# An attention-plus-GLU kernel takes its instruction order and buffer places from a stored table, and most closing waits move ahead of the last four stores

## Chip, cores and metric

The kernel runs on one core of one Trainium2 chip. A core has five engines that each take their instructions in the order of their own queue: TensorE (PE, matrix products), VectorE (DVE), ScalarE (ACT), GpSimd (POOL) and SyncE (SP, which here only starts transfers). They meet through semaphores. The metric is device time in microseconds (us) of one execution; less is better.

## What is computed

Sequence S = 2048, width D = 512, H = 32 heads of 16, feed-forward width F = 1792, all bfloat16.

```python
xn  = layernorm(x)                                   # no scale, no shift
qkv = xn @ wqkv                                      # 512 x 1536
p   = softmax(q @ k.T / 4)                           # per head, 2048 x 2048
a   = (p @ v) @ wo
h   = relu(xn @ W_gate) * (xn @ W_up)
out = x + a + h @ W_down
```

## The kernel before

**Tiles and units.** The 2048 queries are cut into four chunks of 512 (`c4`), the 32 heads into four groups of eight (`gg`), and each group into two blocks of four heads (`ee`). For each of the 32 blocks the kernel walks over 16 key tiles of 128 keys. A key tile of a block is 4 heads x 128 keys x 512 queries of scores. Most key tiles are two *units*: a unit is two heads, whose scores fill two PSUM banks, and one ScalarE instruction (`ACTIVATE ring<-ps`, line 1419) takes the exponential of both banks into a slot of `ring`. There are 720 units. The other 152 key tiles are *quads*: VectorE turns the four banks of scores into integers that are exponentials when they are read as bfloat16 (`qd<-ps`, line 1372), and VectorE or GpSimd makes two shifted copies (lines 1392 and 1388).

**Two halves of TensorE.** Nearly all products use tiles of 64 rows by 32 columns. A *group* is four such instructions side by side in columns, with 512 columns of data, on the upper or the lower 64 rows: half 0 or half 1. All of them are issued by the helper `matmul_loaded` (line 122). The weights of a group are loaded before it by four `LDWEIGHTS` instructions (lines 846, 1324 and 1352), except where the group before it on the same half used the same weights: then the four loads are left out (`wkey`, and `held` in `emit`). The scores of a unit are one group on each half. Behind them in the same queue stand the products with v (`ring,v_aug` and `qd,v_aug`), the projections of q, k and v, the gate, up and down products of the feed-forward part and the output projection.

**Order.** The program is first recorded as a graph of 8,000-odd operations (`Graph.op`). `Graph.run` is a list scheduler: it holds the candidates of each engine, gives each a start time from assumed durations and slacks, and always places the one that can start first, with rules for urgent scores and for weights that can stay. It also gives each tile its buffer (`slot_for`) and puts filler products into idle time at the start. `Graph.emit` then turns dependences into semaphore waits and writes out the five queues in that order.

**Scores and exponentials.** Unit u uses one of two pairs of PSUM banks (`ps`, four banks for units, four for everything else), so its scores have to wait until the exponential of unit u-2 has read them. TensorE can be ahead of ScalarE by one unit, no more.

**End.** SyncE starts all 459 transfers. Each kind of transfer has semaphores of its own, 102 in all. At the end of SyncE's queue `play` waits on every one of them, behind the last four stores (`out_dram<-xn_sb`, line 1221):

```python
            if e == "SP":
                for s, v in fin:
                    eng.wait_ge(s, v)
```

In the compiled program two of these waits share an instruction (line 550, 51 instructions). The output rows of those stores come from a chain behind the last exponential: the last block's sum is normalised on VectorE (lines 1192 to 1199), multiplied by the last part of `wo`, added to the residual (lines 1213 and 1216) and stored.

Of the kernel before, what the change touches and what calls it, by code (L numbers as in the profile page):

```python
# [1 line left out]

# [11 lines left out]
S = 2048  # L14
D = 512
H = 32
DH = 16
F = 1792
# [3 lines left out]
NB = 4  # L22
# [12 lines left out]
D_STEP = 3  # L35
W_LEAD = 34
# [53 lines left out]
NHS = 20  # L90

# [35 lines left out]
class Graph:  # L127
# [67 lines left out]
    def run(self):  # L195
        ops = self.ops
        for o in ops:
            o.users = []
        for o in ops:
            if o.after is not None and int(o.after) > 0:  # L200
                o.order.add(self.units[min(int(o.after), len(self.units)) - 1])
            pre = set(o.deps) | o.order
            o.left = len(pre)
            for d in pre:
                d.users.append(o)
        cand = {e: [] for e in self.ENGS}
        free = {e: 0.0 for e in self.ENGS}
        self.queue = {e: [] for e in self.ENGS}
        for o in ops:
            if o.left == 0:  # L210
                cand[o.eng].append(o)
        n = 0

        def slot_for(t):

            best, second = None, None
            for i in (t.allowed if t.allowed is not None else range(len(t.pool.cur))):
                c = t.pool.cur[i]
                if c is None:
                    at = 0.0  # L220
                else:
                    us = c.w + c.r
                    if not all(u.done for u in us):
                        continue
                    at = max(u.end for u in us)
                if best is None or at < best[0]:
                    best, second = (at, i), best
                elif second is None or at < second[0]:
                    second = (at, i)
            if t.pool.shared:  # L230
                held = any(c is not None and c.open > 0 for c in t.pool.cur)
                if t.extra:
                    if t.extra.slot is None:
                        return None
                elif t.open:
                    if held and not (self.EARLY and second is not None):
                        return None
                elif len(t.allowed) > 3 and (not held or any(b.slot is None and b.extra.slot is not None for b in self.twins)):
                    return second
            return best  # L240


        pe = {"mode": "full", "at": -1e9, "free": [0.0, 0.0]}
        last = {}

        def ready(o):
            at = 0.0
            for d in o.deps:
                at = max(at, d.end if d.eng == "PE" else d.end + ((0.0 if d.urgent else max(self.DMA_SLACK, o.slack)) if d.eng == "SP" else o.slack))
            for d in o.order:  # L250
                at = max(at, d.start if d.eng == o.eng else d.end)
            for t in o.acq:
                if t.slot is not None:
                    continue
                b = slot_for(t)
                if b is None:
                    return None
                at = max(at, b[0] + (o.slack if o.eng == "SP" else 0.0))
            return at

        def pe_start(o, at):

            if o.mode != "half" or pe["mode"] != "half":
                st = max(at, max(pe["free"]) + (self.SWITCH if o.mode != pe["mode"] else 0.0), pe["at"] + self.ISSUE)
            else:
                st = max(at, pe["free"][o.half], pe["at"] + self.ISSUE)
            was = last.get(o.bank) if o.mode == "half" else None
            if was is None or was.half == o.half:
                return st, None
            return max(st, was.end + 25.0), was  # L270

        held = [None, None]

        def pick_pe():
            found = []
            for o in cand["PE"]:
                at = ready(o)
                if at is not None:
                    found.append((pe_start(o, at)[0], o))
            if not found:  # L280
                return None
            urgent = [(st, max(st, free["ACT"] - self.FILL - 60.0) if o.urgent == 2 else ready(o) + 120.0 if o.urgent > 2 else st + 216.0, o) for st, o in found if o.urgent]
            first = min(st for st, o in found)

            def fits(st, o):
                if o.urgent:
                    return True
                for su, by, q in urgent:
                    if o.mode == q.mode and o.half != q.half:
                        if st > by:  # L290
                            return False
                    elif st + o.dur + (self.SWITCH if o.mode != q.mode else 0.0) > by:
                        return False
                return True
            best = None
            for st, o in found:
                if not fits(st, o):
                    continue
                key = (st > first + self.NEAR, st if st > first + self.NEAR else 0.0,
                       o.prio - (self.REUSE if o.half is not None and o.wkey == held[o.half] else 0.0), o.idx)  # L300
                if best is None or key < best[0]:
                    best = (key, st, o)
            return best[1:]


        port = {"DVE": (0.0, None), "POOL": (0.0, None)}

        def pick(e):
            if e == "PE":
                return pick_pe()  # L310
            got = None
            for o in cand[e]:
                at = ready(o)
                if at is None:
                    continue
                at = max(at, free[e])
                if o.port:
                    at = max(at, port["POOL" if e == "DVE" else "DVE"][0])
                late = at > free[e] + 1e-6
                key = (late, at if late else 0.0, o.prio, o.idx)  # L320
                if got is None or key < got[0]:
                    got = (key, at, o)
            return None if got is None else got[1:]

        wire = 0.0
        while n < len(ops):
            best = None
            got_pe = None
            for e in self.ENGS:
                got = pick(e)  # L330
                if e == "PE":
                    got_pe = got
                if got is not None and (best is None or got[0] < best[0]):
                    best = (got[0], e, got[1])
            if got_pe is not None and best[1] == "PE":
                at, o = got_pe
                kind = None
                for f in self.fillers:
                    t = f[0].cur[f[1]]
                    if t is not None and t.name == f[2] and any(u.done for u in t.w):  # L340
                        kind = f
                        break
                if kind is not None:
                    idle = max(pe["free"])
                    before = self.SWITCH if pe["mode"] != kind[4] else 0.0
                    room = at - idle - before - (self.SWITCH if o.mode != kind[4] else 0.0)
                    dur = 216.0 * (self.COLD if idle < self.WARM_AT else 1.0)
                    if room >= dur + 14.0:
                        f = Op()
                        f.eng, f.dur, f.fn, f.prio, f.name, f.mode, f.half, f.bank, f.urgent = "PE", dur, kind[3], 0.0, "fill", kind[4], None, None, 0  # L350
                        f.lat, f.stream, f.after, f.deps, f.order, f.acq, f.users = self.LAT["PE"], None, None, {}, set(), [], []
                        f.load, f.wsrc, f.wkey, f.wwaits, f.pair = None, (), None, (), None
                        f.idx = len(ops) + self.nfill
                        self.nfill += 1
                        f.start = idle + before
                        f.end = f.start + f.dur + f.lat
                        f.done = True
                        f.seq = len(self.queue["PE"])
                        self.queue["PE"].append(f)
                        pe["mode"], pe["at"], pe["free"] = kind[4], f.start, [f.start + f.dur] * 2  # L360
                        continue
# [61 lines left out]
    def emit(self, nc, es):  # L423
# [20 lines left out]
        for e in self.ENGS:  # L444
            n = {}
# [1026 lines left out]
```

## Time and profile before

| what | us |
|---|---|
| median of 3 runs (lowest, highest) | 695.87 (694.74, 700.77) |
| span of the profiled execution | 696.8 |
| first exponential of a unit starts | 11.4 |
| last exponential of a unit starts | 684.2 |
| ACT busy / PE busy / DVE busy / POOL busy | 671.8 / 678.8 / 603.4 / 504.2 |
| weight loads busy (beside PE) | 385.5 |

The profiled execution has no other time on record than its span, which is 0.9 us over the median of the runs and inside their range. In the rows of the profile, "busy" is the union of an engine's instructions; "PEld" is the weight load beside the products; a bracket behind a row gives the idle time ahead of it and what ended it, and "issue" there means that nothing which the profile shows was waited for. A matrix product lasts 375 ns in the rows, but the next group on the same half starts 216 ns after it, since they overlap in the pipeline. The granted TensorE clock is 1.00 in every stretch of the main part.

### The profile page before, as it was taken

To read this page: it belongs to the slowest core of one execution; us is meant where nothing else is said; L and a number is where in the kernel's file an instruction comes from. 1 tells how busy PE (TensorE), PEld (TensorE's weight loads), DVE (VectorE), ACT (ScalarE), POOL (GpSimd) and SP (SyncE) were. 2 spreads that over 40 slices of the span, in tenths; PEclk is the share of its full clock that TensorE was granted. 3 is DMA by queue.
4 is the path that set the end of the run, shared out by engine and by line. 5 is a ranking of instruction groups with operands and counts; after the bars stand their busy time and mean duration, and the time that the engine had idled before them with its cause. 6 is when DMAs were issued, how large, how long until landed. Compare 5 with 4: busy or idle time off the path is not lost.

```text
span 696.8 us, 46210 instructions
## 1 busy us (share of the span) xinstructions
PE 678.8 (97%) x22229; PEld 385.5 (55%) x20884; DVE 603.4 (87%) x1009; ACT 671.8 (96%) x733; POOL 504.2 (72%) x511
## 2 busy tenths in 40 slices
PE   8999999999999999999999999999999999999996
PEld 4556565555654656455655455654655575655663
DVE  9958899999899688888999887899999788899875
ACT  6999999999999999999999999999999999999994
POOL 3323759767689786868979787787778886786871
PEclk9999999999999999999999999999999999999999
DMA  7330312153201121211211121122210121221001
GB/s 212 71 65 6 92 46 63 46 140 96 63 27 40 41 80 55 52 47 56 68 35 33 41 78 49 49 62 58 58 54 25 48 72 50 62 58 40 27 17 48
DMA packets 65736, 40.65 MB, mean 58 GB/s; under 512 B 19912, under 2 KB 61576, under 8 KB 65544
## 3 DMA queue, kind: packets, MB, share of 16 engines
q1 hardware_dynamic: 65544, 37.69, 19.8%
q8 instruction: 169, 2.77, 1.7%
q14 instruction: 23, 0.19, 0.1%
HBM read 31.06 MB, written 2.35 MB: 48 GB/s over the span
## 4 chain that ended last, share of the span: by engine, by line
PE 62%; ACT 33%; DVE 2%; issue 1%; SPq 0%; DMA 0%; DVEq 0%
PE ps L122 61%; ACT ring L1419 32%; DVE qd L1372 1%; PE ps L950 1%; SPq L1288 0%; DVE xn_sb L775 0%; DVE v_aug L911 0%; DMA x_sb<-oT 0%; PE ps L800 0%; ACT qT L993 0%; PE ps L1434 0%; PE ps L968 0%; ACT xnT L808 0%; PE ps L1175 0%; DVEq L552 0%
## 5 line engine op out<-in xcount | busy, mean ns | idle before, releaser
L1419 ACT ACTIVATE ring<-ps 128x1024 bf16<-128x1024 f32 x720 | 665.5, 1102 | 8.5 <-PE ps L122 7.3
L1388 POOL TENSOR_TENSOR qd<-qd,ints 128x512 int32<-128x512 int32 x450 | 454.7, 1042 | 148.8 <-DVE qd L1392 58.7
L122 PE MATMUL ps<-qT,kT 64*32 64x512 bf16 x8192 | 463.5, 375 | 4.1 <-issue 0.9
L1372 DVE TENSOR_SCALAR qd<-ps 128x512 int16<-128x512 f32 x608 | 395.6, 684 | 56.5 <-PE ps L122 51.5
L122 PE MATMUL ps<-qd,v_aug 64*32 64x512 bf16 x3648 | 294.1, 375 | 1.3 <-issue 1.2
L122 PE MATMUL ps<-ring,v_aug 64*32 64x512 bf16 x2880 | 249.9, 375 | 0.5
L1352 PEld LDWEIGHTS <-kT 64*32 64x32 bf16 x7972 | 171.8, 92 | 123.8 <-issue 35.6
L1324 PEld LDWEIGHTS <-v_aug 64*32 64x32 bf16 x5400 | 131.8, 92 | 73.7 <-issue 18.6
L122 PE MATMUL ps<-xnT,wus 64*32 64x512 bf16 x1792 | 138.3, 375 | 1.1 <-issue 1.1
L122 PE MATMUL ps<-xnT,wgs 64*32 64x512 bf16 x1792 | 136.8, 375 | 0.6 <-issue 0.5
L1392 DVE TENSOR_SCALAR qd<-qd 128x2048 int16<-128x2048 int16 x79 | 62.8, 803 | 0.5
L846 PEld LDWEIGHTS <-wgs 64*32 64x32 bf16 x1792 | 44.1, 92 | 26.0 <-issue 5.8
L122 PE MATMUL ps<-Wd,hT 64*32 64x512 bf16 x768 | 56.8, 375 | 1.3 <-DVE qd L1372 0.5
L846 PEld LDWEIGHTS <-hT 64*32 64x32 bf16 x1792 | 44.2, 92 | 23.9 <-issue 4.9
L846 PEld LDWEIGHTS <-wus 64*32 64x32 bf16 x1792 | 44.1, 92 | 24.0 <-issue 5.5
L1057 DVE COPY up_sb<-ps 128x512 f32<-128x512 f32 x56 | 38.2, 683 | 4.6 <-PE ps L122 4.4
L122 PE MATMUL ps<-Wv,hT 64*32 64x512 bf16 x512 | 41.4, 375 | 0.8 <-issue 0.7
L1061 DVE SCALAR_TENSOR_TENSOR hT<-ps,up_sb 128x512 bf16<-128x512 f32 x56 | 38.2, 681 | 4.3 <-PE ps L122 4.0
L122 PE MATMUL ps<-Wk,hT 64*32 64x512 bf16 x512 | 40.5, 375 | 0.0
L122 PE MATMUL ps<-Wo_p,x_sb 64*32 64x512 bf16 x480 | 37.8, 375 | 0.0
L122 PE MATMUL ps<-xnT,Wq 64*32 64x512 bf16 x480 | 36.7, 375 | 0.2 <-issue 0.2
L122 PE MATMUL ps<-xnT,Wk 64*32 64x512 bf16 x480 | 34.2, 375 | 0.2 <-DVE xnT L816 0.2
(72 smaller groups left out, 267.4 us busy)
## 6 DMA issues: line engine op xcount, KB each, us to landing
rb<-rec_scr SPq DMA_DIRECT2D x31, 256.0 KB
wus<-in_B_W_up_dram SPq DMA_DIRECT2D x56, 128.0 KB, 3.1
wgs<-in_B_W_gate_dram SPq DMA_DIRECT2D x56, 128.0 KB, 2.8
xr_sb<-in_A_x_dram SPq DMA_DIRECT2D x16, 128.0 KB, 3.1
out_dram<-xn_sb SPq DMA_DIRECT2D x16, 128.0 KB, 1.8
qT<-qf SPq DMA_DIRECT2D x120, 16.0 KB, 2.8
x_sb<-in_A_x_dram SPq DMA_DIRECT2D x8, 128.0 KB, 2.6
x_sb<-oT SPq DMA_DIRECT2D x60, 16.0 KB, 2.6
```

The source lines that it names most:

```text
L122: return e.add_instruction(mybir.InstMatmult(name=e.bass.get_next_instruction_name(), engine=mybir.EngineType.PE, ins=[e.lower_ap(x), e.lo ...
L846: e.ldweights(w()[rows, 32 * j:32 * j + 32], tile_position=(rows.start, 32 * j))
L950: ins = e.matmul(ps[:, BANK[0], :], Wo_l[:, 0, 0:128], zeros, start=True, stop=True)
L1057: G.op("DVE", 603, lambda e: e.tensor_copy(up_sb[:, tup.slot, :], bank_of(tu)), reads=[tu], writes=[tup], prio=-590)
L1061: G.op("DVE", 603, lambda e: e.scalar_tensor_tensor(out=hT[:, th.slot, :], in0=bank_of(tg), scalar=0.0, in1=up_sb[:, tup.slot, :], op0=ALU ...
L1324: e.ldweights(vs(j), tile_position=(64 * half, 32 * j))
L1352: e.ldweights(ks(m), tile_position=(64 * half, 32 * m))
L1372: G.op("DVE", 601, lambda e, j=j, tx=tx: e.tensor_scalar(qd[:, tq.slot, 512 * j:512 * j + 512], ps[:, BANK[tx.slot], :], IBIAS[3], 0.0, op ...
L1388: G.op("POOL", POOL_NS / POOL_PIECES + 60, lambda e, x=x, n=n, c=slice(i * m, i * m + m): e.tensor_tensor(x().bitcast(I32)[:, c], raw().bi ...
L1392: G.op("DVE", 600, lambda e, n=n, x=x: e.tensor_scalar(x(), raw(), float(SHIFTS[n + 1]), None, op0=ALU.add), reads=[ti, tq], writes=[t], p ...
L1419: exp_ops[u] = G.op("ACT", 904, lambda e, tr=tr, k0=k0: e.activation(ring[:, tr.slot, :, :], ps[:, 4 * k0:4 * k0 + 2, :], ACTF.Exp, scale= ...
```

## The change

The list scheduler in `Graph.run` is taken out. A string of some 14 KB holds, packed, the operation that stands at each of 8,281 places of a common order and the buffer of each tile; `run` unpacks it and fills the five queues from it. No duration, slack or priority is read any more. Dependences that come from buffers being used again are worked out from the table as before; for transfers that share a semaphore, a wait for a user of the one before is added. In `emit`, the closing waits on the transfers that are not among the last four are put ahead of the first of these four.

The graph itself, the kernels' operations, the sizes, the split between engines and the buffers' number are the same. The two compiled programs have the same count of every instruction on ACT, DVE, POOL and SP, and the same matrix products; of weight loads there are 20,764 before and 19,660 after.

```diff
+LAST_STORES = 4
...
+PLAN_OPS = 8281
+PLAN = (
...
     def run(self):
-        ops = self.ops
...
-        def slot_for(t):
...
-        def pick_pe():
...
-        def pick(e):
...
+        ops, n = self.ops, len(self.ops)
+        plain = zlib.decompress(base64.b85decode(PLAN))
+        m = PLAN_OPS
+        self.queue = {e: [] for e in self.ENGS}
+        at, places = -1, iter(plain[2 * m:])
...
+        for i in range(m):
+            at += plain[i] * 256 + plain[m + i] - 65536 * (plain[i] > 127)
+            o = ops[at] if at < n else self.blank(at)
             for t in o.acq:
                 if t.slot is not None:
                     continue
+                t.slot = next(places)
+                c = t.pool.cur[t.slot]
                 if c is not None:
                     for u in c.w + c.r:
+                        assert u in placed
+                        if u.eng != o.eng or o.eng not in ("PE", "ACT"):
                             o.deps[u] = True
+                t.pool.cur[t.slot] = t
+            if o.eng == "SP":
+                for e in self.ENGS:
+                    us = [u for u in users.get(ahead.get(o.stream), ()) if u.eng == e and u is not o and o not in u.deps]
+                    if us:
+                        u = min((u for u in us if u in placed), key=lambda u: u.seq)
+                        if e != "SP":
+                            o.deps[u] = True
+                ahead[o.stream] = o
...
+            o.seq = len(self.queue[o.eng])
+            self.queue[o.eng].append(o)
+            placed.add(o)
         ops += [o for o in self.queue["PE"] if o.name == "fill"]
...
+                if e == "SP" and i == len(self.queue[e]) - LAST_STORES:
+                    late = {id(q.sem[0]) for q in self.queue[e][i:]}
+                    for s, v in fin:
+                        if id(s) not in late:
+                            eng.wait_ge(s, v)
                 wait(o.waits)
                 ins = o.fn(eng)
...
             if e == "SP":
                 for s, v in fin:
-                    eng.wait_ge(s, v)
+                    if id(s) in late:
+                        eng.wait_ge(s, v)
```

## The prediction

> **What bounds the kernel now.** First the page: busy times, instruction queues and the row of the exponentials.
>
> ```profile
> PE 678.8 (97%) x22229; PEld 385.5 (55%) x20884; DVE 603.4 (87%) x1009; ACT 671.8 (96%) x733; POOL 504.2 (72%) x511
> ...
> q8 instruction: 169, 2.77, 1.7%
> ...
> PE 62%; ACT 33%; DVE 2%; issue 1%; SPq 0%; DMA 0%; DVEq 0%
> ...
> L1419 ACT ACTIVATE ring<-ps 128x1024 bf16<-128x1024 f32 x720 | 665.5, 1102 | 8.5 <-PE ps L122 7.3
> ```
>
> ACT and PE both look full, and the chain of waits changes between them. Which of them limits is read from the starts of the 720 exponentials. The first starts at 11.4 us, the last at 684.2: 672.8 us for 719 steps. The commonest and shortest step is 0.904 us, and 719 x 0.904 = 650.0, so ACT is late by 22.8 us in all; 84 steps are over 0.95 us. An order can't shorten the 0.904. It can win back lateness, and something of the 11.4 us ahead or the 12.6 us behind.
>
> Next, where the lateness arises: the timeline around one of the longest pauses.
>
> ```profile
> 152.39 0.10 PEld L846 LDWEIGHTS <-wus 64*32 64x32 bf16 x3
> 152.56 0.38 PE L122 MATMUL ps<-ring,v_aug 64*32 64x512 bf16 x4
> 153.75 0.09 PEld L846 LDWEIGHTS <-wus 64*32 64x32 bf16 x1 [1.26 <-issue]
> 153.75 0.39 PE L122 MATMUL ps<-xnT,wus 64*32 64x512 bf16 x4 [0.81 <-issue]
> ...
> 154.64 1.02 ACT L1419 ACTIVATE ring<-ps 128x1024 bf16<-128x1024 f32 x1 [0.90 <-PE ps L122]
> ```
>
> A group of four weight loads is broken after the third, PE stands still for 1.18 us (152.56 to 153.75) with nothing to wait for, and the next exponential is 0.90 late. Counting PE's rows in the timeline, this pause stands at row 9,150, and every pause of this kind has the same remainder, 190, when its row is divided by 256. The page says why that is no accident: q8 moved 2.77 MB of instructions in 169 packets, PE ran 22,229 + 20,884 = 43,113, so 64 bytes each and one packet per 256. PE pauses where the next packet is not there. The packet ahead of this pause began at 150.89 and had landed at 152.31, and PE went on 1.4 us after that. Over the run PE loses 22.9 us at these borders, 15.05 of them in 25 pauses over 0.3 us. Of ACT's 22.8 us of lateness, 14.1 lie around the 36 pauses over 0.25 us, and 8.7 elsewhere.
>
> Last, the end of SP's queue: the closing waits, and the last four stores.
>
> ```profile
> L550 SPq EVENT_SEMAPHORE  x51: 17/28/28, 693.3 to 696.3; - x51
> ...
> L1221 SPq DMA_DIRECT2D out_dram<-xn_sb x4: 350/442/511, 691.1 to 692.8; - x4
> ...
> DMA to landing us min/median/max: 1.8/1.9/1.9
> ```
>
> 51 instructions from 693.29 to 696.39 are 61 ns each. The last store, issued at 692.77, has landed at about 692.77 + 1.9 = 694.7; the waits go on for 1.7 us after that.
>
> **The change, part by part.**
>
> *Closing waits.* 49 of the 51 instructions go ahead of the first of the last four stores. Queued behind them there are only these four. SP's issue before is at 679.78 (`rb`, line 1271); its landing is what GpSimd's last product (line 1279) waits for, until 684.79. If SP is held that long and then needs 49 x 61 ns = 3.0 us, it is free at 687.8, and the first store's data come at 691.15: 3.3 us of cover. Two instructions are left behind the last landing. Gain 1.7 - 0.1 = **1.6 us**; without the cover, up to 3.0 us would stand ahead of the stores, a loss of 1.4.
>
> *Fewer weight loads.* The change's order lets the same weights stand for two groups more often: 20,764 loads written out become 19,660, so 1,104 instructions or 4.3 packets of 256 less. The loads themselves lie beside products and cost nothing there; what counts is how long a packet lasts. I count matrix products per packet in both orders and set beside it what PE lost in the trace of before:
>
> | products in a packet | before: packets, us lost, pauses over 0.3 us | after: packets |
> |---|---|---|
> | 129 or less | 41, 4.2, 5 | 13 |
> | 130 to 135 | 100, 17.1, 19 | 62 |
> | 136 or more | 21, 1.3, 0 | 82 |
>
> With the same loss per packet in each row, after has 13 x 5/41 + 62 x 19/100 = 13.4 long pauses for 24, and 1.3 + 10.6 + 4.9 = 16.8 us lost for 22.5. Of ACT's 14.1 us near pauses this saves 44% by the number of long ones (6.2 us) or 25% by the sum (3.6 us). I take **6.2 us**, since the lateness was found at long pauses, and keep 0 and 14.1 as bounds.
>
> The page "Runtime: NRT & Kernel Launch" of the Trainium skill ("Instruction fetch mechanics") has blocks of 256 instructions too, but calls the crossing mostly hidden, because dispatch is slower than the fill. By that, this term would be 0 and the time that of the first rival below; the pauses above speak against it.
>
> *Where the groups stand.* Between the scores of one unit and the next, 0.904 us have room for 8.4 groups (216 ns each, two halves). Units with nine or more: 124 before, 200 after, which is worse. Four units in a row with 33 or more: 188 before, 148 after, which is better. Giving each window the mean lateness that such a window has in the trace, ACT's sum goes from 22.4 to 23.6 us by single units, to 22.3 by fours, to 20.7 by eights. I take **0**, and +1.2 and -1.7 as ends.
>
> *Neighbours on the same half.* In program order, 779 groups stand behind one of the same half before, 1,640 after. If the other half may run past a group that waits for its own half, this costs nothing. In the trace it may: of 5,528 groups, 136 begin more than 30 ns before the group that stands ahead of them in the program, 135 of these on the other half. Cost 0; the second rival is the case that it doesn't hold.
>
> *Other queues.* The orders of ACT, of DVE up to its 50th instruction and of PE up to its tenth exponential are the same, so the 11.4 us stay. Products on VectorE's and GpSimd's shifted copies: GpSimd's stand 6 units (before 7) ahead of their reader in the median, 3 (4) at least. Two pieces are 2 x 1.04 us, 2.3 units: still hidden, by less. SP's transfers are mixed anew: gate and up weights now stand at least 8 units, 7.2 us, ahead of their load (up: 10 before), with 3.1 us to landing. The extra waits on transfers with a shared semaphore hold SP only, and fewer of its instructions carry a wait (166, before 208). All of these **0**; if SP is held for the 7.5 to 12.8 us that its longest waits for DVE now take, the weights' cover is gone and a stall of some us follows once or twice. At the end three more groups on half 0 stand behind the last scores, beside 4.4 us in which PE waits for VectorE; bound 3 x 0.216 = 0.6 us.
>
> *Sum*, against the span: 696.8 - 1.6 - 6.2 = 689.0. The runs' median is 0.9 lower: **688.1 us**.
>
> **Rivals.**
>
> *Only the end is faster.* The pauses move to other places and stay as many, for a packet of 136 products lasts 136/8 x 0.216 = 3.7 us at full speed, and one of 132 no less than 3.6. For: four of the long pauses came behind packets that had lasted 3.9 us and more. Against: no long pause in 21 packets of 136 or more. Time 695.9 - 1.6 = 694.3.
>
> *The halves go in program order.* Then a group that waits for its half holds the other half too. Making pairs of neighbours on different halves, the order has 2,920 steps before and 3,052 after, 132 x 0.2155 = 28.4 us more of PE, for 651 us of exponentials a total of 658 us and 16.8 us of pauses. With PE on the chain for 62% of the span, 17.6 us of it reach the end: 695.9 + 17.6 - 1.6 - 6.2 = 705.7; all of it, with no gain at the packets, 722.7. It decides from 7.8 us, 27% of the 28.4. Against are the 136 early groups; for it is that only few places in the trace show it, since before has only half as many such neighbours, and hardly three in a row without a wait. The page "TensorE: Matmul & The Clock Gate" of the Trainium skill ("The mechanism" of tiling) states this rule outright: products start and end strictly in program order, only weight loads are pulled ahead. By it this rival is the forecast; the trace disagrees in the 136.
>
> *Most lateness goes.* Half of the 8.7 us elsewhere go as well, and nearly all of the 14.1: 695.9 - 1.6 - 14.1 - 4.4 = 675.8. For: the order is not bound to starting the earliest first, and no bound stands in the way above 672. Against: pauses can't all vanish with 62 packets in the middle row.
>
> *The waits at the end do harm*, as worked out: 697.3 if nothing else gains.
>
> **How the numbers follow.** Forecast (682 to 692 by its terms' ends around 688) 50%; only the end 18%; program order 16%; most lateness 14%; harm at the end 2%. The range leaves out half of the fourth case at the bottom and most of the second at the top: 676 to 704. One per cent is 7 us, about what a measurement of this kernel can tell from no change: faster means under 688.9, slower over 702.8. Faster: 36 of the forecast's 50 and the 14 of most lateness, 0.50; the same: 14 + 18, and 2 for harm at the end, with 2 of program order, 0.36; slower: 14 of program order, 0.14.
>
> **What will show it.** The waits: two semaphore instructions behind the last landing, the end about 2 us after the last store's issue. The packets: some 165 on q8, and 13 or so pauses over 0.3 us at equal remainders of 256. The halves: if program order rules, PE's rows show the second half starting with the second of two neighbours, and ACT's lateness grows evenly, far from packet borders. Wrong would be the forecast if the exponentials' steps near borders are as late as before, or if ACT waits for DVE or transfers in places where it now doesn't.

## The result and the profile after

The changed kernel is slower by about half a per cent: 699.32 us median of 20 runs (697.04 to 702.00) beside 696.50 of 20 of the kernel before (692.56 to 700.77), ratio 1.0045 with a 95% interval of 1.0029 to 1.0060. Two further measurements, on chips 2 and 14, gave 1.0054 and 1.0050. The forecast was 688.1, so about 11 us are missing; 699.32 lies inside its range, on the side of the second rival. The profiled execution took 700.15 us, with a span of 698.4.

| | before | after |
|---|---|---|
| start to first exponential, us | 11.4 | 11.7 |
| first to last exponential | 672.8 | 675.8 |
| last exponential to end | 12.6 | 10.8 |
| pauses at packet borders: us in all (of these over 0.3 us) | 22.9 (25) | 9.8 (9) |

The end is 1.8 us shorter and the pauses are less than half, and still the stretch of exponentials is 3.0 us longer. First the page of the changed kernel, with the lines that answer to those of before:

```profile
PE 685.9 (98%) x22232; PEld 359.8 (52%) x19780; DVE 598.3 (86%) x1009; ACT 674.8 (97%) x733; POOL 503.2 (72%) x511
...
q8 instruction: 164, 2.69, 1.6%
...
PE 80%; ACT 14%; SPq 2%; DVE 1%; DMA 1%; issue 1%; DVEq 0%
...
L1357 ACT ACTIVATE ring<-ps 128x1024 bf16<-128x1024 f32 x720 | 668.4, 1060 | 8.5 <-PE ps L227 6.7
```

The instruction queue has five packets fewer (169 before). The chain of waits lies on PE for 80% instead of 62%. The idle time ahead of the exponentials is 8.5 us as before, which misleads: the records of two exponentials that follow each other overlap, so an exponential that comes 0.1 us late leaves no idle time at all. Lateness has to be read from their ends (further down). The view of waits gives PE's time without a cause, `issue`: us in all, times, longest. Before and after:

```profile
PE ps L122 <- issue: 5.0, 12, 0.8
```

```profile
PE ps L227 <- issue: 1.0, 3, 0.4
```

That is the saving at the packet borders, as far as this view sees them. And the end of SP's queue, by line (durations in ns, then when the first and the last started):

```profile
L478 SPq EVENT_SEMAPHORE  x48: 28/28/28, 688.2 to 691.1; - x48
...
L1159 SPq DMA_DIRECT2D out_dram<-xn_sb x4: 350/388/437, 694.7 to 696.1; - x4
...
DMA to landing us min/median/max: 1.7/1.8/1.8
...
L488 SPq EVENT_SEMAPHORE  x2: 17/22/28, 697.4 to 697.9; - x2
```

The closing waits end at 691.1, 3.6 us before the first of the last stores; two of them stand behind the last landing. The compiled program packs them into 50 instructions, 51 before; PE, DVE, ACT and GpSimd carry some more semaphore instructions than before too (PE 135, before 116), which e5 below leaves as they are.

### The profile page after: what moved, and what is told of

It is laid out like the page before. It is cut to its first block, busy times and chain, and to the rows that moved or that the text cites. A ratio compares the mean times of both kernels' runs of the same rounds, so it can differ in the third digit from the quotient of the medians.

```text
span 698.4 us, 45138 instructions
## 1 busy us (share of the span) xinstructions
PE 685.9 (98%) x22232; PEld 359.8 (52%) x19780; DVE 598.3 (86%) x1009; ACT 674.8 (97%) x733; POOL 503.2 (72%) x511
## 4 chain that ended last, share of the span: by engine, by line
PE 80%; ACT 14%; SPq 2%; DVE 1%; DMA 1%; issue 1%; DVEq 0%
PE ps L227 79%; ACT ring L1357 14%; DVE qd L1310 1%; SPq L832 1%; DMA wus<-in_B_W_up_dram 1%; SPq L1226 1%; PE ps L888 1%; PE ps L1372 0%; DMA x_sb<-oT 0%; SPq L982 0%; PE ps L738 0%; PE ps L906 0%; ACT xnT L746 0%; DVEq L490 0%; PE ps L1113 0%
## 5 line engine op out<-in xcount | busy, mean ns | idle before, releaser
L227 PE MATMUL ps<-qT,kT 64*32 64x512 bf16 x8192 | 470.8, 374 | 2.0 <-issue 0.6
L227 PE MATMUL ps<-qd,v_aug 64*32 64x512 bf16 x3648 | 265.8, 375 | 0.1
L227 PE MATMUL ps<-ring,v_aug 64*32 64x512 bf16 x2880 | 242.2, 375 | 0.7 <-issue 0.4
L1290 PEld LDWEIGHTS <-kT 64*32 64x32 bf16 x7560 | 158.0, 92 | 123.0 <-issue 37.3
L1262 PEld LDWEIGHTS <-v_aug 64*32 64x32 bf16 x4708 | 113.4, 91 | 77.1 <-issue 25.1
L784 PEld LDWEIGHTS <-hT 64*32 64x32 bf16 x1792 | 41.3, 92 | 29.3 <-issue 6.5
L1330 DVE TENSOR_SCALAR qd<-qd 128x2048 int16<-128x2048 int16 x79 | 53.9, 690 | 0.5
L227 PE MATMUL ps<-Wv,hT 64*32 64x512 bf16 x512 | 46.2, 375 | 0.1
L227 PE MATMUL ps<-Wk,hT 64*32 64x512 bf16 x512 | 44.7, 375 | 0.0
```

The lines of the kernel that those rows point to most:

```text
L227: return e.add_instruction(mybir.InstMatmult(name=e.bass.get_next_instruction_name(), engine=mybir.EngineType.PE, ins=[e.lower_ap(x), e.lo ...
L784: e.ldweights(w()[rows, 32 * j:32 * j + 32], tile_position=(rows.start, 32 * j))
L1262: e.ldweights(vs(j), tile_position=(64 * half, 32 * j))
L1290: e.ldweights(ks(m), tile_position=(64 * half, 32 * m))
L1330: G.op("DVE", 600, lambda e, n=n, x=x: e.tensor_scalar(x(), raw(), float(SHIFTS[n + 1]), None, op0=ALU.add), reads=[ti, tq], writes=[t], p ...
```

## The experiments

Ratios are to the kernel before on the same chip; 1% is 7 us. "Late" is, of one profiled execution, the sum over the 719 steps from the end of one exponential to the end of the next, less 0.9165 us each (the last section says where that comes from), "near" what of it lies up to some 4 us behind pauses over 0.25 us at packet borders (with a stretch of 2 us, up to 2 us of it would count as "elsewhere" instead).

| kernel | chip | ratio to before (95%) | late, us: near + elsewhere | pauses, us (over 0.3) |
|---|---|---|---|---|
| before | | 1 | 11.2 + 2.8 | 22.9 (25) |
| after | | 1.0045 (1.0029 to 1.0060) | 4.1 + 12.8 | 9.8 (9) |
| e1_waits_alone | 2 | 0.9983 (0.9965 to 1.0001) | 10.3 + 2.1 | 20.8 (26) |
| e2_loads_back | 2 | 1.0108 (1.0077 to 1.0140) | 2.4 + 16.6 | 8.8 (8) |
| e3_cap9 | 2 | 1.0043 (1.0023 to 1.0062) | 3.8 + 17.0 | 7.9 (6) |
| e4_halves | 2 | 1.0081 (1.0055 to 1.0107) | 4.9 + 15.7 | 11.5 (13) |
| e5_interleave | 12 | 0.9964 (0.9940 to 0.9989) | 3.0 + 8.3 | 8.9 (8) |
| e6_transfers | 12 | 0.9998 (0.9978 to 1.0019) | 5.1 + 10.2 | 9.8 (9) |
| e7_both | 12 | 0.9893 (0.9861 to 0.9925) | 1.5 + 5.7 | 6.9 (6) |
| e8_more_transfers | 9 | 0.9942 (0.9927 to 0.9957) | 0.9 + 3.8 | 4.9 (3) |
| e9_before_interleave | 9 | 0.9975 (0.9960 to 0.9991) | 4.2 + 2.8 | 11.5 (11) |
| e10_both_loads_back | 9 | 0.9999 (0.9984 to 1.0014) | 2.2 + 5.8 | 8.6 (9) |
| e11_before_fewer_loads | 2 | 0.9908 (0.9893 to 0.9922) | 4.3 + 2.9 | 10.8 (11) |
| e12_more_transfers_loads_back | 2 | 0.9951 (0.9933 to 0.9969) | 8.6 + 5.6 | 20.1 (22) |
| e13_more_transfers_again | 2 | 0.9929 (0.9905 to 0.9952) | 5.9 + 4.5 | 13.7 (16) |
| e14_changed_again | 2 | 1.0054 (1.0038 to 1.0069) | 5.2 + 12.2 | 11.6 (12) |
| e15_changed_once_more | 14 | 1.0050 (1.0029 to 1.0071) | 4.0 + 13.1 | 7.1 (5) |
| e16_interleave_again | 14 | 0.9969 (0.9946 to 0.9993) | 4.1 + 9.0 | 9.9 (13) |
| e17_both_again | 14 | 0.9926 (0.9898 to 0.9954) | 1.4 + 5.3 | 6.7 (7) |
| e18_both_loads_back_again | 14 | 0.9992 (0.9967 to 1.0017) | 5.2 + 7.9 | 14.7 (18) |

**One part at a time.** e1 is the kernel before with nothing but its closing waits moved:

```diff
+LAST_STORES = 4
...
+                if e == "SP" and i == len(self.queue[e]) - LAST_STORES:
+                    late = {id(q.sem[0]) for q in self.queue[e][i:]}
+                    for s, v in fin:
+                        if id(s) not in late:
+                            eng.wait_ge(s, v)
```

> The order of before, with the move of the closing waits alone. All theories expect the same of it: the stores stay where they are, two semaphore instructions are left behind the last landing, and the span ends about 2.3 us behind the last store's issue, where it took 4.0 us: 1.6 to 1.7 us less, 0.9977 of before. If the waits have no cover, the last stores come later instead: up to 1.4 us more, 1.002.

0.9983, or 1.2 us; the term of the sum was 1.6. The interval reaches 1.0001, so the runs alone hardly tell it from nothing, but in the trace the stretch from the last exponential to the end is 11.0 us instead of 12.6. Its lateness is about that of before.

e2 is the changed kernel with 276 of its 613 kept weights loaded again, 1,104 instructions, as many as before:

```diff
             if held[o.half] == o.wkey:
+                stay += 1
+                if stay * 276 // 613 > (stay - 1) * 276 // 613:
+                    continue
                 o.load, o.wsrc = False, ()
```

> The changed kernel's order, but in 276 of its 613 places where a weight is kept for a second group it is loaded again, so that the weight loads are as many as before (20,764), at the same products in the same order. If the fewer loads saved lateness (the packets' theory), the long pauses at packet borders go from 9 back to some 20 or 25, ACT's lateness near them from 4.6 us to 10 to 14, and the time rises by 5 to 9 us over the changed kernel, to 704 to 708 us. If the pauses hardly matter, because what is lost there would be lost elsewhere, the time stays within 1 us of the changed kernel's 699.3.

1.0108, where the changed kernel on that chip had 1.0054: the fewer loads are worth 0.54% here, 3.8 us. So most of the gain that was forecast is there in the time, and something else takes more than it. The trace of e2 does not show how: its pauses sum to 8.8 us (8 over 0.3 us) where 20 to 25 long ones had been expected, and only 2.4 of its 19.0 us of lateness lie near them. It is the second quickest execution of six (702.09 us; four took 705.6 to 706.5), and no slower one was profiled. The loads themselves cost nothing where they stand: at the 276 places the time from the group ahead on the same half is that of the changed kernel, 0.2 us more over all of them.

**Crowding and runs, two theories that fell.** e3 moves the scores of 88 units ahead in the table, so that fewer steps have nine or more groups. Here and below, an edit of the table is shown by the places where it first differs, of PE's order as half and product:

```diff
-1 xnT,Wk
 0 qT,kT
 1 qT,kT
+1 xnT,Wk
```

> The changed kernel's order, with the scores of 88 units moved ahead so that no more than 9 groups of products stand between the scores of one unit and the next (79 units have ten or eleven in the changed kernel); weight loads 19,728 for 19,660. If crowding between successive scores makes the lateness (units of nine or more: 12.8 us of the 25.9), that lateness falls by 3 to 6 us and the time to 693 to 696 us. If it is runs of groups on one half of PE, or the other queues, that make it, the time stays at 698 to 701 us.

1.0043, the ratio of the changed kernel (1.0054 on that chip), and 20.8 us of lateness, no less than there, in an execution that was the slowest of nine. How crowded single steps are was not it.

e4 moves 153 groups so that fewer stand in runs of three or more on one half (250 runs became 141):

```diff
 1 Wv,xnT
 0 Wv,xnT
+1 Wv,xnT
 0 Wv,xnT
-1 Wv,xnT
 0 qT,kT
```

> The changed kernel's order, with 153 groups moved a few places so that runs of three and more groups on one half of PE fall from 250 to 141 (128 before); how many groups stand between the scores of successive units, and the weight loads, are as in the changed kernel. If PE looks only about one group ahead, so that a run of three on one half leaves the other half idle, ACT's lateness falls by 2 to 5 us and the time to 694 to 697 us. If crowding or the other queues make the lateness, the time stays at 698 to 701 us.

1.0081, no gain and perhaps a loss (the changed kernel on that chip 1.0054, intervals that meet). Counting runs was the wrong measure; what e4 left in place is told below.

**The order between the halves.** e5 merges the halves by the time at which each group can start when neither half waits for the other, reckoned with the durations of the trace. Each half's own sequence, the 19,660 loads and the other four queues are as in the changed kernel, and only how the two sequences are merged into PE's one queue differs: in 1,154 places of PE, one of them here:

```diff
 0 qT,kT
-0 ring,v_aug
-0 ring,v_aug
 1 qT,kT
+0 ring,v_aug
+0 ring,v_aug
```

> The changed kernel with nothing but PE's program order altered: the sequence of groups on each half of PE, the weight loads (19,660), and the orders of all other queues stay, and only the way in which the two halves' sequences are interleaved is put in the order in which the groups could start if no half ever waited for the other (1,154 of PE's places differ; runs of three and more on one half 250 to 94, groups without a neighbour on the other half 576 to 312, which is before's number). If PE's short look-ahead across halves makes the lateness that is spread evenly over the run, 6 to 9 us of ACT's lateness go, and the time is 690 to 694 us. If crowding between scores or the other queues make it, the sequences on the halves are as they were and the time stays at 698 to 701 us.

0.9964. The place of the diff, in the timeline (start, duration, and behind `x` the instructions, four to a group), in the changed kernel:

```profile
631.70 0.41 PE L227 MATMUL ps<-qT,kT 64*32 64x512 bf16 x8
631.92 0.60 PE L227 MATMUL ps<-ring,v_aug 64*32 64x512 bf16 x8
...
632.60 1.02 ACT L1357 ACTIVATE ring<-ps 128x1024 bf16<-128x1024 f32 x1 [0.19 <-PE ps L227]
```

and in e5:

```profile
626.20 0.41 PE L228 MATMUL ps<-qT,kT 64*32 64x512 bf16 x8
626.41 0.60 PE L228 MATMUL ps<-ring,v_aug 64*32 64x512 bf16 x8
...
625.78 2.04 ACT L1358 ACTIVATE ring<-ps 128x1024 bf16<-128x1024 f32 x2
```

PE's rows are the same: the two groups of scores start 0.03 us apart, so in the changed kernel the score on half 1 does run past the two products on half 0 that stand ahead of it in the program. But its exponential starts 0.87 us behind that score, 0.30 us late, and in e5 (the second of the two in the row, at 626.69) 0.46 us behind it and on time. The trace also keeps the time of each semaphore increment, from which the views name what ended a wait, and there is the difference. In the changed kernel the score on half 1 signals its end at 632.58, 0.84 us after its start and 0.04 behind the signal of the second product (632.53); in e5 at 626.64, 0.41 after its start.

The same holds over the whole run. A group that signals does so 0.40 us after its start in the median. With the trace's groups matched to the program's order, in none of ten traces (before, after, e4 to e7, e9 and e14 to e16; some 3,090 signals each) does a group signal ahead of one that stands before it in the program, and signals are at least 0.042 us apart. A group that has run past others signals about 0.44 us after the last of these has started. That holds back the signals of 131 scores in the changed kernel, by 20.8 us in all (130 and 20.3 in e15), of 18 in before (2.5 us), of 34 in e5 (3.8), and of 122 in e4 (19.3). Not every such delay reaches ACT.

What reaches ACT can be read step by step. Fifty-two of the 719 steps are late in all three executions of the changed kernel and less late in both of e5's program: together 7.1 to 7.7 us in the former and 0.3 in the latter. Executions that had no part in choosing them agree: 7.7 in e6, which has the changed kernel's order of PE, and 0.3 or less in e7 and e17. In 19 of the 52 (3.1 us) it is the signal that is late, as shown; in the other 33 the signal follows the score's start by the usual 0.40 to 0.46 us, so the score itself started late, and what made it late is not split further. Over the run the steps that are late by 0.02 to 0.4 us far from pauses fall from 77 (9.3 us) to 35 (4.2 us). ACT's lateness falls by 5.6 us, a little less than the 6 to 9 expected.

e9 is the control: the order of before, its waits moved as in e1, merged by the same rule. Only 98 places of PE differ from before, two of them here:

```diff
 0 xnT,Wk
-0 xnT,Wk
 1 Wv,xnT
+0 xnT,Wk
 0 qT,kT
```

> A control: the order of the kernel before (every queue and every buffer place), written as a table into the changed kernel, with its closing waits, and PE's halves interleaved by the same rule as in the experiment on interleaving. In that order only 98 of PE's places differ (1,154 in the changed kernel's), so by the theory of the short look-ahead there is nothing to win, and the time is that of the kernel before with the closing waits alone, 695 to 697 us. If interleaving by start helps for another reason, or the way the table is played makes a difference of its own, it is under 693 or over 698.

0.9975, as e1 within the intervals: the list scheduler's order, which always placed what could start first, stood nearly in that order already, with 18 held scores that become 7.

**The transfers.** In the changed kernel SP's queue stands behind `rec_scr<-rrec` (line 1206) until VectorE has made `rrec`; the view of waits has 4.5 us there, from 339.8 on. Then the timeline of SP:

```profile
344.33 0.34 SPq L1206 DMA_DIRECT2D rec_scr<-rrec  x1
344.71 0.52 SPq L1226 DMA_DIRECT2D x_sb<-oT  x1
345.27 0.58 SPq L982 DMA_DIRECT2D wus<-in_B_W_up_dram  x1
...
350.77 0.83 SPq L982 DMA_DIRECT2D wus<-in_B_W_up_dram  x1
```

and of PE, 5 us behind the last of these:

```profile
354.39 0.59 PE L227 MATMUL ps<-qd,v_aug 64*32 64x512 bf16 x8
355.77 0.39 PE L227 MATMUL ps<-xnT,wus 64*32 64x512 bf16 x4 [0.79 <-DMA wus<-in_B_W_up_dram]
```

The second load of `wus` is issued at 350.77, seven other transfers behind the first, and PE stands idle for 0.79 us until it has landed; ACT loses 1.4 us there. There are four large stalls in this trace (at 354, 386 to 389, 420 and 594 to 601 us; 1.4, 1.4, 0.55 and 1.9 us). e6 moves 34 transfers ahead by one to eleven places in SP's queue and leaves PE's order as it is:

```diff
 x_sb<-oT
 wus<-in_B_W_up_dram
+wus<-in_B_W_up_dram
 qT<-qf
...
-wus<-in_B_W_up_dram
```

> The changed kernel with nothing but SP's order altered: 34 transfers whose data land within 2 us of their reader's turn, and whose buffer had been free for a while, go 1 to 11 places ahead in SP's queue, past transfers that wait or are needed later. If late transfers make the few large stalls (354 us: 1.4 us of lateness, 386 to 389: 1.4, 420: 0.55, 594 to 601: 1.9), 3 to 5 us go and the time is 694.5 to 696.5 us. If these stalls are made by PE's order or by the packets, the time stays at 698 to 701 us.

0.9998, and SP's timeline shows that second load next to the first:

```profile
345.37 0.34 SPq L1206 DMA_DIRECT2D rec_scr<-rrec  x1
345.75 0.52 SPq L1226 DMA_DIRECT2D x_sb<-oT  x1
346.31 1.10 SPq L982 DMA_DIRECT2D wus<-in_B_W_up_dram  x2
```

The stalls at 354 and 386 us are gone (in e16 both stay, in e5 the first). The one at 420 stays at 0.5 us in e6 and is gone in e5 and e16, so it was the order of the halves. Of the one at 594 to 601, e6 keeps 1.9 us; what is left of it in e7 stands at 587 us there.

e7 has both edits (1,161 places of PE, merged anew for the earlier transfers). Its diff is those of e5 and e6 together.

> Both edits: SP's order as in the kernel with the moved transfers, and PE's two halves interleaved anew on top of it (1,161 places). If look-ahead and transfers are both causes, their savings add: 9 to 13 us, to 686 to 690 us, 8 us below the kernel before. If only one of them is, the time is that of the better of the two alone; if neither, 698 to 701 us.

0.9893 on the chip of e5 and e6, 689.9 us. Its exponentials wait for half as long as before:

```profile
L1358 ACT ACTIVATE ring<-ps 128x1024 bf16<-128x1024 f32 x720 | 663.2, 1078 | 4.0 <-PE ps L228 3.8
```

e8 moves 59 more transfers ahead, and four stores of finished rows back (PE's order, merged anew, differs in ten places), since e7 has one stall of 1.45 us left, at 587 us:

```diff
-wgs<-in_B_W_gate_dram
+wus<-in_B_W_up_dram
+wus<-in_B_W_up_dram
 rb<-rec_scr
```

> The kernel with both edits, and SP's order moved further: transfers with less than 4.5 us between landing and reader go ahead where they can, and the four stores of finished output rows at 578 to 602 us go back by 3 to 14 places. In the kernel with both edits the largest lateness left is 1.45 us at 587 us, where PE waits for VectorE, which may be behind a transfer issued at 584.5. If so, 1 to 2 us go: 688 to 689 us. If VectorE is late there by its own work, the time stays at 689.5 to 690.5.

> The kernel with both edits and the further moved transfers once more, as the pair of the one with the loads put back. On the chip where before ran in 692 us it was at 0.994 of before. If the share of the packets differs by chip, then on a chip where before runs in 697 us the ratio is 0.986 to 0.989, and the time again 688 to 690 us.

e13 is e8 again. 0.9942 and 0.9929 on two chips: under both kernels, but no gain over e7 (0.9893 and 0.9926), where 0.986 to 0.989 had been expected of e13. The stall at 587 us is gone, and e8's trace has the least lateness of all.

**What the fewer loads are worth.** e10 is e7, e12 is e8, each with the edit of e2. e11 is e9 with the weights of 276 more groups left out:

```diff
+                if held[o.half] is not None and o.name.startswith("pv"):
+                    gone += 1
+                    if gone % 4 == 0 and gone // 4 <= 276:
+                        o.load, o.wsrc = False, ()
```

> The kernel with both edits, and 276 of its 613 kept weights loaded again, so that the loads are as many as before (20,764). If fewer loads save pauses at packet borders, these pauses come back where hardly another lateness is left to hide them: 4 to 7 us more than with both edits alone, 694 to 697 us, and the pauses' sum goes from 6.9 us to 12 to 20. If the loads cost nothing, 689 to 691 us.

> The control kernel (order of before, closing waits moved), with 276 groups' weight loads left out: products of the probabilities with the values use the weights that stood on their half, so the output is not the reference's; 19,660 loads instead of 20,764, all products stay. If the loads' packets make most of the lateness in the order of before, the time falls by 3 to 6 us under the control's ratio of 0.9975 to 0.998, to 0.989 to 0.994 of before. If not, it stays at 0.997 to 0.999.

> The kernel with both edits and the further moved transfers, and 276 of its 613 kept weights loaded again (20,764 loads). By the packets' theory 2 to 6 us more than its pair without the loads in this batch, the less the fewer pauses the kernel before has on this chip; if loads cost nothing, within 1 us of the pair.

e10 has 0.9999, 691.7 us, where 694 to 697 had been expected; but on its chip before itself runs in 692.0. Beside e8 on that chip, which has other transfers, it is 3.9 us slower. Its pauses sum to 8.6 us where 12 to 20 had been expected, against 4.9 in e8.

e11, the order of before with 1,104 loads less, has 0.9908 where e1 on that chip had 0.9983: 5.2 us, or 4.7 against e9's 0.9975 on another chip, whose order of PE it has. Its pauses are 10.8 us, e1's 20.8. The view of waits gives PE's time without a cause in e12 and, with 1,104 loads less, in e13:

```profile
PE ps L228 <- issue: 4.2, 11, 0.7
```

```profile
PE ps L228 <- issue: 1.3, 2, 1.0
```

The pauses go from 20.1 to 13.7 us with them, but the ratio only from 0.9951 to 0.9929, 1.5 us where 2 to 6 had been expected, with intervals that overlap.

**All on one chip.** Up to here the order, the transfers and the loads had been measured on different chips, and before itself had 692.0 us on chip 9 and 697 on the others. So the changed kernel (again in e14 beside e12 and e13), e5, e7 and e10 ran once more, without a new edit, beside each other:

> The changed kernel once more, on the same chip as the others of this batch: 1.0045 of before on a chip like the one it was first timed on; 1.008 to 1.011 where before runs in 692 us, since the pauses that its fewer loads save are fewer there.

> The changed kernel again, so that the order and the transfers can be compared with it on one chip; until now they were compared through the kernel before on different chips. Ratio to before 1.003 to 1.007, as in both earlier measurements (1.0045 and 1.0054). If the chip matters for the order's loss, it is outside this.

> Only the program order of the two halves of TensorE is changed against the changed kernel. Theory (a group that waits for its half holds the other): 5 us or more under the changed kernel of the same chip, ratio to before about 0.996 to 0.999. Rival (the 5.6 us found before are a difference between chips): within 2 us of the changed kernel.

> Order of the halves and 34 transfers moved ahead together. Theory (both losses add up to at least their sum): 8 to 11 us under the changed kernel of the same chip and 3 or more under the kernel with the order alone, ratio to before 0.987 to 0.995. Rival (the ratio of 0.989 found before owes to that chip): not more than 6 us under the changed kernel.

> The kernel with both edits, with 276 of the 613 kept weights loaded again (1,104 instructions, 4.3 packets more). If fewer loads are worth 4 to 5 us in this order too: 4 to 7 us over the kernel with both edits on the same chip. If they are worth 1 to 2 us there, as the last such pair said: 1 to 2 us over it.

Chip 14 (before 695.77 us): changed 1.0050, with the order of the halves 0.9969 (5.6 us less), with the transfers as well 0.9926 (3.0 us less again), with the loads back 0.9992 (4.6 us more). "Elsewhere" goes from 13.1 to 9.0 and to 5.3 us on the way.

## Why the prediction failed

Term by term, in us; minus is a gain:

| term | predicted | measured | from |
|---|---|---|---|
| *Closing waits* | -1.6 | -1.2 | e1 |
| *Fewer weight loads* | -6.2 | -3.8, -5.2, -4.6, -1.5 | e2 and e14; e11 and e1; e18 and e17; e12 and e13 |
| *Neighbours on the same half* | 0 | +5.6, +5.6 | after and e5; e15 and e16 |
| *Other queues* | 0 | +3.3, +3.0 | after and e6; e16 and e17 |

With -4.5 for the loads the terms make +3.0, with the mean of the four pairs, -3.8, +3.7; measured are +2.8 by the medians.

*Closing waits*: right, with its mechanism. Cover and landing came as worked out: free at 691.1 with 3.6 us to spare (predicted 3.3), two instructions left, the end 2.3 us behind the last issue (predicted about 2).

*Fewer weight loads*: right in kind, a little too large. Lateness near pauses fell from 11.2 to 4.1, 5.2 and 4.0 us in three executions, and 164 packets and 9, 12 and 5 long pauses came where 165 and 13 were forecast. In the time it is 0.5 to 0.75% in three of four pairs and 0.2% in the last, so 4 to 5 us in most where 6.2 were forecast. That the gain comes through the pauses is what four pairs of traces show (before and after, e1 and e11, e17 and e18, e13 and e12); e2's trace doesn't, so how e2 loses its 3.8 us stays open. The page "Runtime: NRT & Kernel Launch" of the Trainium skill ("Instruction fetch mechanics"), which calls the crossing mostly hidden, does not hold for this kernel: before loses 22.9 us at 169 borders, and e11, the order of before with loads left out, gains 5.2 us.

*Neighbours on the same half*, "Cost 0", is the first step that failed. The 136 early groups were read as proof that a half may run past a group that waits for the other at no cost. They prove only that it may start. What ACT waits for is the signal at the end, and the signals keep the program's order: in the changed kernel 484 of 5,528 groups begin more than 30 ns early, but none signals early, and the order across the halves costs 5.6 us. The page "TensorE: Matmul & The Clock Gate" of the Trainium skill ("The mechanism") states that products start and end strictly in program order; the 484 early starts go against its letter, the 3,095 signals of this trace agree with it for the ends.

So the second rival named the right cause in part. Its mechanism, that a group which waits for its half holds the other half, is not what the starts show: where such a group has no semaphore to wait for and the next group, on the other half, could start over 0.06 us earlier, the next one did so in 259 of 267 places of the changed kernel. A group whose semaphore comes last does hold the other half: in 105 such places the next group never started before it. But e5 has 110 of these and before 52, so they are not what e5 gained. The rival's price was three times too high (17.6 us), and 5.6 is under the 7.8 from which it was to decide. What it was to show, lateness in small even steps far from borders, is what the trace has (77 steps of 0.02 to 0.4 us, 9.3 us, where before has 21 and 2.2). What stays open is why the scores at the other 33 steps start late.

*Other queues*, "0", is the second. The prediction named the condition itself, SP held for long and the cover of the weights gone, "a stall of some us follows once or twice", and then left it out of the sum. The longest single waits were no guide: the stall shown came behind a wait of 4.5 us, and it was the ten issues from the end of that wait to the load (344.33 to 350.77, 6.4 us) that used up the rest of the cover.

*Where the groups stand*, 0: e3 agrees, as far as steps with nine groups or more go.

The measure was off as well. 719 x 0.904 = 650.0 us was taken for the least that ACT needs, and so 22.8 us for lateness, of which 8.7 elsewhere. The least is 719 x 0.9165 = 659.0; 9 us of the "lateness" were ACT's own pace, and before had only some 3 elsewhere. With all of before's 14.0 us of lateness gone and the gain at the end, 695.9 - 14.0 - 1.6 = 680.3 would be the least, so the third rival, *Most lateness goes*, could not have come at its 675.8; and the false measure hid how good the order of before already was away from the borders. The share of the chain, by which the second rival was scaled, is no scale either: PE has 80% of it in the changed kernel, 79% in e17, which is 8.6 us faster, and 54% in e7, the same program as e17. Their lines of the page, e17 and e7:

```profile
PE 79%; ACT 19%; DVE 1%; issue 1%; DVEq 0%
```

```profile
PE 54%; ACT 42%; DVE 2%; DMA 1%; issue 1%; POOLq 0%; POOL 0%; DVEq 0%
```

With both failed terms mended, e17 and e7 lie at 0.9926 and 0.9893; the forecast was 688.1/695.87 = 0.9888. That e7 comes so near it is partly luck: the two terms that were forecast came smaller, -1.2 and about -4.5 us, and would make 0.992.

## What to carry to other kernels

A stored order is only as good as what its search counts as late: two queues that share one instruction stream need a common order by the time at which each can start, even where the trace shows that one starts ahead of the other. An event seen in a trace (a group that starts early) bounds nothing; before a term is set to zero, look at what the consumer waits for (here the end's signal, not the start), and at whether that comes early too. And for each transfer, count the issues between the last long wait ahead of it on its queue and itself, not only the units of cover to its reader.

## What was unexpected of the hardware

ACT's pace: exponentials on time *start* 0.904 us apart, but each record is 12.5 ns longer than the one before it (1.018 us up to some 1.2), so their *ends* never come closer than 0.910 in any trace and lie 0.917 apart in the median. A row of ACT's timeline in e7, 13 exponentials without idle time between them (start, duration, count), gives the pace: the first takes 1.02, the other ends follow in (12.02 - 1.02)/12 = 0.917 us each.

```profile
588.68 12.02 ACT L1358 ACTIVATE ring<-ps 128x1024 bf16<-128x1024 f32 x13 [1.34 <-PE ps L228]
```

Pauses at the packet borders differ between executions of the same program: e8 lost 4.9 us at them on chip 9 and 13.7 on chip 2 (as e13), the kernel of e10 8.6 on chip 9 and 14.7 on chip 14 (as e18). Before runs in 692.0 us on chip 9 and in 695.8 to 697.5 on the others, which goes with it.

Early starts on TensorE without early ends: the signals of groups on the two halves keep the program's order in each of the ten traces named above, however far one group starts ahead.

An issue on SP is not always half a microsecond: most take 0.35 to 0.6 us, but 53 of the 467 in the changed kernel over 1 us, up to 2.0.
